# A Fourier mixing and MLP mixer kernel: the setup in a new order

## The chip, the cores and the metric

The kernel runs on one core of a Trainium2 chip. The metric is the device time of one execution in microseconds (us); the shown time is the median of several. The core has five engines that work side by side, each through its own instructions in order: TensorE (PE in the profile, with PEld for its weight loads), VectorE (DVE), ScalarE (ACT), GpSimd (POOL) and SyncE (SP). PE writes its products to PSUM, a small memory of which a DVE or ACT instruction carries them to SBUF, where all tiles lie. Transfers between SBUF and HBM are issued by POOL (with a cast from fp32 to fp16 here) or by SP.

## What is computed

```python
def _attn_ref(x):                      # x: 8 x 3008 x 256
    X = np.fft.fft(x, axis=1)
    X = np.fft.fft(X, axis=2)
    return X.real.astype(np.float32)

def _moe_ref(x, w_tok1, w_tok2, w_ch1, w_ch2):
    xt = x.transpose(0, 2, 1)
    h = np.maximum(xt @ w_tok1, 0.0) @ w_tok2
    u = x + h.transpose(0, 2, 1)
    h2 = np.maximum(u @ w_ch1, 0.0) @ w_ch2
    return (u + h2).astype(np.float32)
```

For each of 8 batches the input (3008 tokens by 256 features) goes through a two-dimensional Fourier transform, of which the real part is kept. The result goes through a token MLP (3008 to 256 to 3008, ReLU between) with a residual, and a channel MLP (256 to 1536 to 256) with a residual.

## The kernel before

**The stages of a batch.** The transform over 3008 = 47 x 64 tokens and 256 features is done by matmuls with tables of cosines and sines. `load_x` brings a batch to SBUF as `xp`, and its mirror image, by two gathers with computed row numbers, as `xm`. `fold` (DVE) adds and subtracts the mirrored halves, so that real tables suffice: xp += xm, then `eo`. It does so in four pieces of four token positions; feature 0 has two operations of its own (L426, L427). `front` is the rest of the Fourier stage and the token MLP. First `pz` (tables `t1n`, `t1b`, copied to `z`), then twelve groups of `pw` (tables `td0`, `td1`, combined to `w`), then `tok1` for each half of the 256 hidden tokens (`pt`, against `hp` and `hq`), then `third`: the last Fourier stage, by the tables `tp` and `tq`, in three chunks of 512 tokens, giving `yt`. Last `pu`, the second token matrix, whose sum with `yt` is `ut`, the input of the channel MLP. `mm1` (`pc`, copied to `c1` with the ReLU) and `mm2` (`po`, or `px` and `py` with sums of blocks that save a matmul) are the channel MLP. SP turns `ut` for the residual (`rt`) and stores the output `osb`.

**The order is written by hand.** The program has a manual schedule: each engine gets its instructions in the order of the program text. `front` and `fold` are generators, and `take(g, n)` puts the next n pieces of one into the text. After the setup a loop over batches and chunks weaves the channel MLP of one batch with the `front` of the next and the `fold` of the one after that. The lists `plan`, `own_plan` and `fold_at` say how many pieces go where.

**The setup.** Before the loop there is a stretch of some 38 us in which all tables are computed on the chip, the weights arrive, batch 0 is folded and taken through its `front`, and the first token matrix is carried into the transform's domain: `carried` multiplies `w1p` and `w1m` by the turned tables (`tts_p`, `tts_q`) and gives `hp` and `hq` (`ph`). This is the part of interest:

- POOL's iotas give `pcol` (the partition number), `ix8f`, `krow`, `kb` and `jrow`. `krow` and `kb` are generated between the two gathers of batch 0, `jrow` behind them.
- DVE makes from `pcol` a set of one-column values (`reff`, `offp`, `offq` and others). With them `kb` becomes the arguments of the angle tables, reduced to a period (`reduced`: add and subtract 2 to the 23rd). ACT takes the sines. `tp` (from `mp`) is reduced on DVE. `tq` (from `mq`) and the `td` tables (from `md`) are begun on ACT, by Identity with a scale and a bias, and ended by one DVE operation each (on `vq` and `vd`).
- `turn` transposes a table on PE, with copies on ACT to `tt`; `turn_rows` reverses its rows with a matmul by `anti` (`pr`), again copied by ACT.
- `filler(n)` issues n matmuls of 128 columns on PE whose result nobody reads.
- The weights follow batch 0 on POOL's queue: `w1p`, `w1m` twice, `w2s` (w_tok2), `wc1` (w_ch1, once straight and once by a gather with the index `ixc`); after the setup come batch 1 (`load_x(1)`) and last `wc2` (w_ch2, `load_wc2`).

At the end of the setup, these are the lines that set the order:

```python
    turn(tp, tts_p, 8)
    table3(tq, vq)
    turn_rows(tts_p, 1.0, 0)
    pieces = fold(0, [nc.vector] * 4)
    take(pieces, 3)
    table_d()
    take(pieces, 9)
    turn(tq, tts_q, 4)
    own = front(0)
    take(own, 4)
    turn_rows(tts_q, -1.0, 24)
```

`relu(0, tok1(0))`, `tok1(1)` and `third(0, ...)` are the three pieces of `front` between the pw groups and the first `pu`. `tok1(0)` also contains a small matmul with `perm` (L492), whose result ACT writes into column 131 of `w`; `third` reads this column.

Of the kernel before, what the change touches and what calls it, by code (L numbers as in the profile page):

```python
# [40 lines left out]
def kernel(  # L41
# [61 lines left out]
    iota(ix8f[:], [[376, BB], [1, 2]], 374, 0)  # L103
    rowi = pvec("rowi")
# [5 lines left out]
    ixc = const.tile([P, 1], I32, tag="ixc")  # L110
    cfeat = pvec("cfeat")
    ts(cfeat[:], pcol[:], 1.0, AT.is_lt, -128.0, AT.mult)
    ts(cfeat[:], cfeat[:], 256.0, AT.add)
    nc.vector.tensor_tensor(out=ixc[:], in0=cfeat[:], in1=pcol[:], op=AT.subtract)
# [7 lines left out]
    def load_x(b, between=(None, None)):  # L122
# [10 lines left out]
        for k in range(2):  # L133
            if between[k] is not None:
                between[k]()
            gather(xmf[:, 8 * D * k:8 * D * (k + 1)], x8, ix8[0:KG, b, k:k + 1])
# [9 lines left out]
    krow = gen.tile([P, 4, 24], FP32, tag="krow")  # L146
    jrow = gen.tile([P, 129], FP32, tag="jrow")
    kb = gen.tile([P, 768], FP32, tag="kb")

    def rows1():  # L150
        iota(krow[:], [[0, 4], [1, 24]], 0, 0)

    def rows3():
        iota(kb[:].rearrange("p (g k) -> p g k", g=NG), [[2, NG], [47, 64]], 0, 0)


# [4 lines left out]
    for t in (tp, tq):  # L161
        for i in range(2):
# [9 lines left out]
    x_tiles = {0: load_x(0, (rows1, rows3))}  # L172
    iota(jrow[:], [[1, 129]], 0, 0)
# [23 lines left out]
                                   op0=AT.mult, op1=AT.add)  # L197

# [38 lines left out]
    def reduced(m, period, nrow, width, eng=nc.vector):  # L237

        v = gen.tile([P, width], FP32, tag="gv", bufs=2, name="gv")[0:nrow, :]
        eng.tensor_scalar(out=v, in0=m, scalar1=1.0 / period, scalar2=TWO23,  # L240
                          op0=AT.mult, op1=AT.add)
        eng.tensor_scalar(out=v, in0=v, scalar1=-TWO23, scalar2=-float(period),
                          op0=AT.add, op1=AT.mult)
        r = gen.tile([P, width], FP32, tag="gr", bufs=2, name="gr")[0:nrow, :]
        eng.tensor_tensor(out=r, in0=v, in1=m, op=AT.add)
        return r

    def sin(out_, in_, scale):
        nc.scalar.activation(out=out_, in_=in_, func=AFT.Sin, scale=scale)

    def table3(tab, r):
        for i in range(2):
            h = slice(64 * i, 64 * i + 64)
            sin(tab[h, :, h], r[h, :].rearrange("p (g k) -> p g k", g=NG), PI2 / S)
# [25 lines left out]
    def filler(n):  # L280
        pw = ps_out("filler")
        for _ in range(n):
            nc.tensor.matmul(pw[:, 0:P], lhsT=ident[:], rhs=anti[:], start=True,  # L283
                             stop=True)
# [9 lines left out]

    mask0, q24 = pvec("mask0"), pvec("q24")
# [4 lines left out]
    m1 = gen.tile([P, 120], FP32, tag="m1")  # L300
    kf = krow[:].rearrange("p a k -> p (a k)")
    ts(m1[0:KR, 0:48], kf[0:KR, 0:48], qcol[0:KR, :], AT.mult, 47 / 4, AT.add)
    ts(m1[0:KR, 48:96], kf[0:KR, 48:96], qcol[0:KR, :], AT.mult)
    ts(m1[0:KR, 96:120], kf[0:KR, 0:24], q24[0:KR, :], AT.mult, 47 / 8, AT.add)
    r1 = reduced(m1[0:KR, :], 47, KR, 120)
    cs = gen.tile([P, 120], FP32, tag="cs")
    sin(cs[0:KR, :], r1, PI2 / 47)

    up, down = pvec("up"), pvec("down")
    nc.vector.memset(up[:], TWO23)
    nc.vector.memset(down[:], -TWO23)
    mp, mq, vq = (gen.tile([P, 768], FP32, tag=n, name=n) for n in ("mp", "mq", "vq"))
    for o, i, scale, bias in ((mq, kb, reff[:], offq), (vq, mq, 1.0 / S, up),
                              (vq, vq, 1.0, down)):
        nc.scalar.activation(out=o[:], in_=i[:], func=AFT.Identity, scale=scale,
                             bias=bias[:])
    ts(mp[:], kb[:], reff[:], AT.mult, offp[:], AT.add)  # L320
    table3(tp, reduced(mp[:], S, P, 768))

    ident = const.tile([P, P], FP16, tag="ident")
    anti = const.tile([P, P], FP16, tag="anti")
    acol = pvec("acol")
    ts(acol[:], pcol[:], -1.0, AT.mult, 127.0, AT.add)
    ts(ident[:], jrow[:, 0:P], pcol[:], AT.is_equal)
    ts(anti[:], jrow[:, 0:P], acol[:], AT.is_equal)

    csv = cs[0:KR, 0:96].rearrange("p (a b k) -> p a b k", a=2, b=2)  # L330
    for i, m in ((0, mask0), (1, xicol)):
        ts(t1n[:, :, i, :], csv[:, :, i, :], m[0:KR, :], AT.mult)
    ts(t1b[:, 1, :], cs[0:KR, 96:120], float(np.sqrt(0.5)), AT.mult,
# [392 lines left out]
    def take(g, n):  # L726
        for _ in range(n):
            next(g, None)
# [132 lines left out]
```

## Time and profile before

| | |
|---|---|
| median of 6 runs | 610.98 us (610.37 to 612.6) |
| the profiled execution | 610.4 us |
| its span, first to last instruction | 608.6 us |
| mean granted PE clock | 0.999 |
| PE busy | 588.2 us (97%) |
| DVE busy | 453.6 us (75%) |
| ACT busy | 442.2 us (73%) |
| POOL busy | 150.5 us (25%) |
| first matmul of PE | 11.69 us after the start of the span |
| first matmul of the second Fourier stage (pw) of batch 0 | 24.99 us |
| HBM read, written | 34.98 MB, 24.64 MB |

Times in the profile are counted from the first instruction of the profiled execution (the span's start); this execution took 1.8 us more than its span. An engine's busy time says little by itself: what counts is which engine others wait for. So the profile also has, for each group of instructions, the idle time of its engine just before it and what ended that ("<-ACT tp L249": until that instruction of ACT was done), and the chain of work that ended last, followed back from the end. "L249" is line 249 of the kernel. A line can be that of a helper: all `tensor_scalar` instructions made through `ts` have L87 or L89, all copies made through `copy` L288 or L290.

### The profile page before, as it was taken

The page shows a single profiled execution, that of the slowest core. Times are in us where ns is not written, and L with a number is a line of the kernel's source. Part 1 is how long each engine was busy: PE and PEld are TensorE (multiplying, and loading weights), DVE is VectorE, ACT ScalarE, POOL GpSimd, SP SyncE. Part 2 cuts the span into 40 slices and gives each one's busy share as a digit, 9 for nine tenths or more (in the row PEclk, how much of TensorE's full clock was granted, in tenths as well). Part 3 has the DMA queues.
Part 4 walks back from the last instruction along what each step waited for, and adds up shares of the span by engine and source line. Part 5 has one row for each costly group of instructions (what it writes and reads, how often), then busy time and mean ns, then how long its engine had stood idle before and what let it go on. Part 6 is the DMA issues. An engine that isn't in the chain of part 4 may idle for free.

```text
span 608.6 us, 15700 instructions
## 1 busy us (share of the span) xinstructions
PE 588.2 (97%) x6322; PEld 422.1 (69%) x6322; DVE 453.6 (75%) x1014; ACT 442.2 (73%) x996; POOL 150.5 (25%) x235
## 2 busy tenths in 40 slices
PE   2899999999999999999999999999999999999996
PEld 1766667666777668767777767766687667766675
DVE  8669679658987697757988688846979676666672
ACT  8866886677768777687777777677776877767672
POOL 8500423112243113401314222311131112111131
PEclk9999999999999999999999999999999999999999
DMA  8994963735548423672329333392231423242423
GB/s 139 210 192 89 180 74 67 150 55 86 62 80 155 84 53 73 112 125 53 84 57 174 57 86 72 70 185 53 53 70 48 95 53 81 61 70 60 90 58 100
DMA packets 86601, 56.53 MB, mean 93 GB/s; under 512 B 54864, under 2 KB 83472, under 8 KB 85776
## 3 DMA queue, kind: packets, MB, share of 16 engines
q1 hardware_dynamic: 78048, 37.84, 32.2%
q0 software_dynamic: 8256, 17.49, 16.7%
q8 instruction: 49, 0.80, 0.5%
q10 hardware_dynamic: 224, 0.20, 0.1%
q14 instruction: 24, 0.20, 0.1%
HBM read 34.98 MB, written 24.64 MB: 98 GB/s over the span
## 4 chain that ended last, share of the span: by engine, by line
PE 92%; DVE 4%; ACT 3%; issue 1%; DVEq 0%; POOL 0%; POOLq 0%
PE pc L592 39%; PE px L633 23%; PE py L633 9%; PE pu L552 7%; PE po L690 4%; PE pt L488 3%; PE pz L445 2%; PE py L519 1%; PE pq L519 1%; PE pw L472 1%; PE pw L473 1%; DVE sb L609 1%; PE filler L283 1%; DVE w L475 1%; DVE xp L423 0%
## 5 line engine op out<-in xcount | busy, mean ns | idle before, releaser
L595 ACT ACTIVATE c<-pc 128x512 f16<-128x512 f32 (+1 forms) x572 | 295.8, 594 | 39.5 <-PE pc L592 19.9
L618 POOL TENSOR_TENSOR osb<-osb,rt 128x256 f32<-128x256 f32 x84 | 81.2, 966 | 377.3 <-DVE osb L618 360.6
L592 PE MATMUL pc<-ut,wc1p 128*128 128x512 f16 x576 | 140.3, 379 | 0.0
L633 PEld LDWEIGHTS <-c 128*128 128x128 f16 x2016 | 121.4, 98 | 20.4 <-DVE c L609 0.3
L592 PE MATMUL pc<-ut,wc1m 128*128 128x512 f16 (+1 forms) x576 | 134.9, 370 | 0.0
L560 DVE TENSOR_TENSOR ut<-pu,yt 128x512 f16<-128x512 f32 (+1 forms) x96 | 64.6, 674 | 51.3 <-PE pu L552 51.1
L633 PEld LDWEIGHTS <-sb 128*128 128x128 f16 x1512 | 89.8, 98 | 10.3 <-issue 0.7
L638 ACT ACTIVATE m<-px 128x256 f32<-128x256 f32 x126 | 48.5, 385 | 66.1 <-PE px L633 38.0
L592 PEld LDWEIGHTS <-wc1p 128*128 128x128 f16 x576 | 52.2, 98 | 49.0 <-issue 2.2
L592 PEld LDWEIGHTS <-wc1m 128*128 128x128 f16 x576 | 53.0, 98 | 46.4
L633 PE MATMUL px<-wst,c 128*128 128x128 f16 x1008 | 70.8, 219 | 0.2 <-DVE c L609 0.2
L633 PE MATMUL px<-wc,c 128*128 128x128 f16 x1008 | 63.1, 219 | 0.0
L290 ACT ACTIVATE z<-pz 128x480 f16<-128x480 f32 (+1 forms) x60 | 40.0, 672 | 18.0 <-PE pz L445 11.0
L609 DVE TENSOR_TENSOR sb<-sb,c 128x768 f16<-128x768 f16 x84 | 50.3, 598 | 2.9
L618 DVE TENSOR_TENSOR osb<-py,m 128x256 f32<-128x256 f32 x84 | 35.2, 420 | 21.9 <-ACT m L638 20.0
L609 DVE TENSOR_TENSOR sb<-c 128x768 f16<-128x768 f16 x84 | 48.9, 582 | 2.3 <-ACT c L595 2.3
L475 DVE SCALAR_TENSOR_TENSOR w<-alt,pw 128x131 f16<-128x131 f16 x96 | 33.1, 350 | 22.9 <-ACT w L290 22.4
L552 PE MATMUL pu<-w2p,uu 128*128 128x512 f16 (+1 forms) x168 | 50.0, 379 | 0.0
L609 DVE TENSOR_TENSOR sb<-c,sb 128x768 f16<-128x768 f16 x84 | 47.1, 561 | 0.0
L609 DVE TENSOR_TENSOR c<-c 128x768 f16<-128x768 f16 x84 | 46.6, 554 | 0.0
L526 DVE TENSOR_TENSOR yt<-py,qs 128x512 f16<-128x512 f32 x48 | 30.9, 686 | 14.3 <-ACT qs L522 14.2
L633 PE MATMUL py<-wst,sb 128*128 128x128 f16 x504 | 35.2, 219 | 0.2 <-DVE sb L609 0.2
(163 smaller groups left out, 687.7 us busy)
## 6 DMA issues: line engine op xcount, KB each, us to landing
out_dram<-osb SPq DMA_DIRECT2D x83, 256.0 KB, 3.5
xp<-in_x_dram POOLq DMA_DIRECT2D x16, 272.0 KB
out_dram<-osb SPq DMA_DIRECT2D x11, 192.0 KB, 3.2
xp<-in_x_dram POOLq DMA_DIRECT2D x16, 127.5 KB
rt<-ut SPq DMA_TRANSPOSE x96, 3.6
w2s<-in_moe_w_tok_dram POOLq DMA_DIRECT2D x1, 1504.0 KB
w1p<-in_moe_w_tok_dram POOLq DMA_DIRECT2D x2, 384.0 KB
wc<-in_moe_w_ch_dram POOLq DMA_DIRECT2D x1, 768.0 KB
```

Source lines behind the costliest of these rows:

```text
L290: nc.scalar.activation(out=out_, in_=in_, func=AFT.Copy)
L475: nc.vector.scalar_tensor_tensor(out=w[:, g, 0:131], in0=alt[:], scalar=pw[:, 131:132], in1=pw[:, 0:131], op0=AT.mult, op1=AT.add)
L526: nc.vector.tensor_tensor(out=yt[:, h, CW * c:CW * c + CW], in0=py[:], in1=qs[:], op=op)
L552: nc.tensor.matmul(pu[:, 0:n], lhsT=uu[:, th, int(minus), h, :], rhs=w2_cols(b, c)[:, th], start=(th == 0), stop=(th == 1))
L560: nc.vector.tensor_tensor(out=ut[:, h, 0:n].rearrange("p (a b) -> p a b", b=64), in0=pu[:, 0:n].rearrange("p (b a) -> p a b", b=64), in1=y ...
L592: nc.tensor.matmul(pc[:, 0:n], lhsT=wc[:, h, ct * P:(ct + 1) * P], rhs=ut[:, h, 0:n], start=(h == 0), stop=(h == 1))
L595: nc.scalar.activation(out=c1[:, ct, 0:n], in_=pc[:, 0:n], func=AFT.Relu)
L609: nc.vector.tensor_tensor(out=o, in0=x, in1=y, op=op)
L618: eng.tensor_tensor(out=o, in0=x, in1=y, op=AT.add)
L633: nc.tensor.matmul(o[:, t], lhsT=a(k)[:, f:f + P], rhs=w(k), start=(first and t == 0 and k == 0), stop=(k == HC - 1), skip_group_check=True)
L638: nc.scalar.activation(out=m[:, i], in_=pa[:, 0], func=AFT.Copy)
L690: nc.tensor.matmul(po[0:n, o:o + D], lhsT=c1[:, ct, ks * P:ks * P + n], rhs=wc2[:, ct, :], start=(ct == 0), stop=(ct == NCT - 1))
```

## The change

The setup is re-planned in these points:

- `krow` and `kb` are gone. `jrow` (0 to 128) is generated ahead of batch 0's transfers, and all tables are computed from it: `mp` by one `scalar_tensor_tensor` from two broadcast inputs, `mq` by ACT as `mp` plus a column `dq`. The gathers follow each other without an iota between them.
- `md` and `vd` are computed and reduced on DVE instead of ACT; `table_d()` goes ahead of the turning, so that ACT has the sines of `cs`, `tp`, `tq` and `td` one behind the other.
- `fold` begins with the two operations of feature 0, which read all of `xm` (both gathers). This holds for every batch.
- `turn(tq, ...)` comes behind the first two pieces of `front(0)`. In the copies of batch 0's `z`, one of the second stretch's and one of the third's, and both of the last ones, are on DVE.
- Fillers: none behind `turn_rows(tts_q, ...)` (24 before), none between the pz pieces (4 before), then 8 instead of 12, and 12 instead of 24 at the end.
- For batch 0 the `perm` matmul (`mirrored`) is issued ahead of `tok1(0)`, and `third(0)` stands between `tok1(0)` and `tok1(1)`, with the PSUM tiles of `mirrored` and `tok1(1)` in another pool. The other batches keep the old order.
- `load_wc2()` comes ahead of `load_x(1)`.

```diff
--- before.py
+++ after.py
...
+    jrow = const.tile([P, 129], FP32, tag="jrow")
+    iota(jrow[:], [[1, 129]], 0, 0)
...
-    ixc = const.tile([P, 1], I32, tag="ixc")
-    cfeat = pvec("cfeat")
-    ts(cfeat[:], pcol[:], 1.0, AT.is_lt, -128.0, AT.mult)
-    ts(cfeat[:], cfeat[:], 256.0, AT.add)
-    nc.vector.tensor_tensor(out=ixc[:], in0=cfeat[:], in1=pcol[:], op=AT.subtract)
...
-    def load_x(b, between=(None, None)):
+    def load_x(b):
...
-            if between[k] is not None:
-                between[k]()
...
-    krow = gen.tile([P, 4, 24], FP32, tag="krow")
-    jrow = gen.tile([P, 129], FP32, tag="jrow")
-    kb = gen.tile([P, 768], FP32, tag="kb")
-    def rows1():
-        iota(krow[:], [[0, 4], [1, 24]], 0, 0)
-    def rows3():
-        iota(kb[:].rearrange("p (g k) -> p g k", g=NG), [[2, NG], [47, 64]], 0, 0)
...
-    x_tiles = {0: load_x(0, (rows1, rows3))}
-    iota(jrow[:], [[1, 129]], 0, 0)
+    x_tiles = {0: load_x(0)}
...
-    def reduced(m, period, nrow, width, eng=nc.vector):
-        v = gen.tile([P, width], FP32, tag="gv", bufs=2, name="gv")[0:nrow, :]
-        eng.tensor_scalar(out=v, in0=m, scalar1=1.0 / period, scalar2=TWO23,
-                          op0=AT.mult, op1=AT.add)
-        eng.tensor_scalar(out=v, in0=v, scalar1=-TWO23, scalar2=-float(period),
-                          op0=AT.add, op1=AT.mult)
-        r = gen.tile([P, width], FP32, tag="gr", bufs=2, name="gr")[0:nrow, :]
-        eng.tensor_tensor(out=r, in0=v, in1=m, op=AT.add)
-        return r
-    def sin(out_, in_, scale):
-        nc.scalar.activation(out=out_, in_=in_, func=AFT.Sin, scale=scale)
+    def reduced(v, r, m, period):
+        ts(v, m, 1.0 / period, AT.mult, TWO23, AT.add)
+        ts(v, v, -TWO23, AT.add, -float(period), AT.mult)
+        nc.vector.tensor_tensor(out=r, in0=v, in1=m, op=AT.add)
+    def sin(out_, in_, period):
+        nc.scalar.activation(out=out_, in_=in_, func=AFT.Sin, scale=PI2 / period)
...
-            sin(tab[h, :, h], r[h, :].rearrange("p (g k) -> p g k", g=NG), PI2 / S)
+            sin(tab[h, :, h], r[h, :, :], S)
...
-            nc.tensor.matmul(pw[:, 0:P], lhsT=ident[:], rhs=anti[:], start=True,
+            nc.tensor.matmul(pw[:, 0:P], lhsT=ident[:], rhs=ident[:], start=True,
...
+    dq, r2, r47 = (pvec(n) for n in ("dq", "r2", "r47"))
+    nc.vector.tensor_tensor(out=dq[:], in0=offq[:], in1=offp[:], op=AT.subtract)
+    ts(r2[:], reff[:], 2.0, AT.mult)
+    ts(r47[:], reff[:], float(NQ), AT.mult)
+    gp = gen.tile([P, NG], FP32, tag="gp")
+    mp, vp, mq, vq = (gen.tile([P, NG, 64], FP32, tag=n, name=n)
+                      for n in ("mp", "vp", "mq", "vq"))
+    up, down = pvec("up"), pvec("down")
+    nc.vector.memset(up[:], TWO23)
+    nc.vector.memset(down[:], -TWO23)
+    ts(gp[:], jrow[:, 0:NG], r2[:], AT.mult, offp[:], AT.add)
+    nc.vector.scalar_tensor_tensor(
+        out=mp[:], in0=jrow[:, 0:64].unsqueeze(1).to_broadcast([P, NG, 64]),
+        scalar=r47[:], in1=gp[:].unsqueeze(2).to_broadcast([P, NG, 64]),
+        op0=AT.mult, op1=AT.add)
+    ixc = const.tile([P, 1], I32, tag="ixc")
+    cfeat = pvec("cfeat")
+    ts(cfeat[:], pcol[:], 1.0, AT.is_lt, -128.0, AT.mult)
+    ts(cfeat[:], cfeat[:], 256.0, AT.add)
+    nc.vector.tensor_tensor(out=ixc[:], in0=cfeat[:], in1=pcol[:], op=AT.subtract)
+    for o, i, scale, bias in ((mq, mp, 1.0, dq), (vq, mq, 1.0 / S, up),
+                              (vq, vq, 1.0, down)):
+        nc.scalar.activation(out=o[:], in_=i[:], func=AFT.Identity, scale=scale,
+                             bias=bias[:])
+    ident = const.tile([P, P], FP16, tag="ident")
+    ts(ident[:], jrow[:, 0:P], pcol[:], AT.is_equal)
+    anti = const.tile([P, P], FP16, tag="anti")
+    acol = pvec("acol")
+    ts(acol[:], pcol[:], -1.0, AT.mult, 127.0, AT.add)
+    ts(anti[:], jrow[:, 0:P], acol[:], AT.is_equal)
...
-    m1 = gen.tile([P, 120], FP32, tag="m1")
-    kf = krow[:].rearrange("p a k -> p (a k)")
-    ts(m1[0:KR, 0:48], kf[0:KR, 0:48], qcol[0:KR, :], AT.mult, 47 / 4, AT.add)
-    ts(m1[0:KR, 48:96], kf[0:KR, 48:96], qcol[0:KR, :], AT.mult)
-    ts(m1[0:KR, 96:120], kf[0:KR, 0:24], q24[0:KR, :], AT.mult, 47 / 8, AT.add)
-    r1 = reduced(m1[0:KR, :], 47, KR, 120)
-    cs = gen.tile([P, 120], FP32, tag="cs")
-    sin(cs[0:KR, :], r1, PI2 / 47)
-    up, down = pvec("up"), pvec("down")
-    nc.vector.memset(up[:], TWO23)
-    nc.vector.memset(down[:], -TWO23)
-    mp, mq, vq = (gen.tile([P, 768], FP32, tag=n, name=n) for n in ("mp", "mq", "vq"))
-    for o, i, scale, bias in ((mq, kb, reff[:], offq), (vq, mq, 1.0 / S, up),
-                              (vq, vq, 1.0, down)):
-        nc.scalar.activation(out=o[:], in_=i[:], func=AFT.Identity, scale=scale,
-                             bias=bias[:])
-    ts(mp[:], kb[:], reff[:], AT.mult, offp[:], AT.add)
-    table3(tp, reduced(mp[:], S, P, 768))
-    ident = const.tile([P, P], FP16, tag="ident")
-    anti = const.tile([P, P], FP16, tag="anti")
-    acol = pvec("acol")
-    ts(acol[:], pcol[:], -1.0, AT.mult, 127.0, AT.add)
-    ts(ident[:], jrow[:, 0:P], pcol[:], AT.is_equal)
-    ts(anti[:], jrow[:, 0:P], acol[:], AT.is_equal)
-    csv = cs[0:KR, 0:96].rearrange("p (a b k) -> p a b k", a=2, b=2)
+    m1 = gen.tile([KR, 5, 24], FP32, tag="m1")
+    for a, n, col, off in ((0, 2, qcol, 47 / 4), (2, 2, qcol, 0.0), (4, 1, q24, 47 / 8)):
+        ts(m1[:, a:a + n, :], jrow[0:KR, 0:24].unsqueeze(1).to_broadcast([KR, n, 24]),
+           col[0:KR, :], AT.mult, off, AT.add)
+    cs, v1 = (gen.tile([KR, 5, 24], FP32, tag=n, name=n) for n in ("cs", "v1"))
+    reduced(v1[:], m1[:], m1[:], 47)
+    sin(cs[:], m1[:], 47)
+    reduced(vp[:], vp[:], mp[:], S)
+    table3(tp, vp)
+    nc.vector.scalar_tensor_tensor(out=vq[:], in0=vq[:], scalar=-float(S), in1=mq[:],
+                                   op0=AT.mult, op1=AT.add)
+    table3(tq, vq)
...
-        ts(t1n[:, :, i, :], csv[:, :, i, :], m[0:KR, :], AT.mult)
-    ts(t1b[:, 1, :], cs[0:KR, 96:120], float(np.sqrt(0.5)), AT.mult,
+        ts(t1n[:, :, i, :], cs[:, i:4:2, :], m[0:KR, :], AT.mult)
+    ts(t1b[:, 1, :], cs[:, 4, :], float(np.sqrt(0.5)), AT.mult,
...
-    quarter = pvec("quarter")
-    nc.vector.memset(quarter[:], 64.0)
-    nc.scalar.activation(out=md[:, 0:128], in_=jrow[:, 1:129], func=AFT.Identity,
-                         scale=pcol[:], bias=quarter[:])
-    nc.scalar.activation(out=md[:, 128:255], in_=jrow[:, 1:128], func=AFT.Copy,
-                         scale=pcol[:])
-    for i, scale, bias in ((md, 1.0 / 256, up), (vd, 1.0, down)):
-        nc.scalar.activation(out=vd[:], in_=i[:], func=AFT.Identity, scale=scale,
-                             bias=bias[:])
+    ts(md[:, 0:128], jrow[:, 1:129], pcol[:], AT.mult, 64.0, AT.add)
+    ts(md[:, 128:255], jrow[:, 1:128], pcol[:], AT.mult)
+    reduced(vd[:], md[:], md[:], 256)
...
-    nc.vector.scalar_tensor_tensor(out=vq[:], in0=vq[:], scalar=-float(S), in1=mq[:],
-                                   op0=AT.mult, op1=AT.add)
...
     def table_d():
-        nc.vector.scalar_tensor_tensor(out=vd[:], in0=vd[:], scalar=-256.0, in1=md[:],
-                                       op0=AT.mult, op1=AT.add)
-        sin(td0[:, 2:130], vd[:, 0:128], PI2 / 256)
-        sin(td1[:, 1:P], vd[:, 128:255], PI2 / 256)
+        sin(td0[:, 2:130], md[:, 0:128], 256)
+        sin(td1[:, 1:P], md[:, 128:255], 256)
...
-            tt(out=xp[:, t, 1:D], in0=xp[:, t, 1:D], in1=xm[0:KR, rv, D - 1:0:-1], op=add)
-            yield
-            if t0 == 1:
+            if s == 0:
...
+            tt(out=xp[:, t, 1:D], in0=xp[:, t, 1:D], in1=xm[0:KR, rv, D - 1:0:-1], op=add)
+            yield
+            if t0 == 1:
...
-                copy(b == 0 and t0 < 2 + 5 * half, zo[:, :, :, t0:t0 + 5],
+                copy(b == 0 and half and t0 < 11, zo[:, :, :, t0:t0 + 5],
...
-            copy(b == 0 and half, zo, pz[:, 0:96].rearrange("p (u k) -> p u k", u=4))
+            copy(b == 0, zo, pz[:, 0:96].rearrange("p (u k) -> p u k", u=4))
...
+        def mirrored(pt):
+            nc.tensor.matmul(pt[:, 260:260 + NG], lhsT=perm[:], rhs=w[:, :, 130],
+                             start=True, stop=True)
+            nc.scalar.activation(out=w[:, :, 131], in_=pt[:, 260:260 + NG],
+                                 func=AFT.Copy)
         def tok1(th):
...
-            pt = ps_f("pt1")
+            pt = (ps_f if b or th == 0 else ps_out)("pt1")
...
-            if th == 0:
-                nc.tensor.matmul(pt[:, 260:260 + NG], lhsT=perm[:], rhs=w[:, :, 130],
-                                 start=True, stop=True)
-                nc.scalar.activation(out=w[:, :, 131], in_=pt[:, 260:260 + NG],
-                                     func=AFT.Copy)
+            if th == 0 and b:
+                mirrored(pt)
...
-        relu(0, tok1(0))
-        yield
-        uv1 = tok1(1)
-        yield
-        third(0, (1, uv1))
-        yield
+        if b:
+            relu(0, tok1(0))
+            yield
+            uv1 = tok1(1)
+            yield
+            third(0, (1, uv1))
+            yield
+        else:
+            mirrored(ps_out("pt1"))
+            uv0 = tok1(0)
+            yield
+            third(0, (0, uv0))
+            yield
+            relu(1, tok1(1))
+            yield
...
+    table_d()
     turn(tp, tts_p, 8)
-    table3(tq, vq)
     turn_rows(tts_p, 1.0, 0)
-    pieces = fold(0, [nc.vector] * 4)
-    take(pieces, 3)
-    table_d()
-    take(pieces, 9)
+    take(fold(0, [nc.vector] * 4), 12)
+    own = front(0)
+    take(own, 2)
...
-    own = front(0)
...
-    turn_rows(tts_q, -1.0, 24)
+    turn_rows(tts_q, -1.0, 0)
...
-    filler(4)
-    take(own, 2)
-    filler(12)
+    filler(8)
...
     for g2 in range(2):
...
     take(own, 5)
-    filler(24)
+    filler(12)
+    load_wc2()
...
-    load_wc2()
...
```

More of the change, by code (lines that the diff above doesn't have):

```diff
@@ L422, in fold @@
             rv = slice(16 - t0, 16 - t1 if t1 < 17 else None, -1)
+            if s == 0:
+                tt(out=xp[:, 1:NR, 0], in0=xp[:, 1:NR, 0], in1=xm[0:KR, ::-1, 0], op=add)
+                tt(out=eo[:, :, 0], in0=xp[:, :, 0], in1=xp[:, :, 0], op=add)
             tt(out=xp[:, t, 1:D], in0=xp[:, t, 1:D], in1=xm[0:KR, rv, D - 1:0:-1], op=add)
@@ L425, in fold @@
             if t0 == 1:
-                tt(out=xp[:, 1:NR, 0], in0=xp[:, 1:NR, 0], in1=xm[0:KR, ::-1, 0], op=add)
-                tt(out=eo[:, :, 0], in0=xp[:, :, 0], in1=xp[:, :, 0], op=add)
                 t = slice(0, t1)
```

## The prediction

> **What bounds the kernel.** I read four views: the page's slices, its chain of waits, the list of waits of TensorE (PE), and the timelines of the engines up to 60 us.
>
> ```profile
> PE   2899999999999999999999999999999999999996
> ...
> PE 92%; DVE 4%; ACT 3%; issue 1%; DVEq 0%; POOL 0%; POOLq 0%
> ```
> The first line is PE's busy share in 40 slices of 15.2 us, the second the share of the chain that ended last. PE is saturated from slice 3 on. The waits of PE after 64 us agree; the first of these two lines is the largest of them, and the other is the largest of the start:
>
> ```profile
> PE pt L488 <- DVE w L475: 0.7, 1, 0.7
> ...
> PE pt L265 <- ACT tp L249: 11.7, 1, 11.7
> ```
> (waiter, releaser, us in total, times, longest.) So whatever shortens the start reaches the end whole, and nothing else in this change can bring much: the change adds no arithmetic after the start. The start is a relay of the engines, each in its own order:
>
> ```profile
> 11.69 1.46 PE L265 MATMUL pt<-ident,tp 128*128 128x128 f16 x12 [11.69 <-ACT tp L249]
> 17.17 1.44 PE L265 MATMUL pt<-ident,tq 128*128 128x128 f16 x12 [1.19 <-ACT tt L275]
> 21.43 1.50 PE L283 MATMUL filler<-anti,ident 128*128 128x128 f16 x24
> 24.99 0.23 PE L472 MATMUL pw<-td,z 128*128 128x128 f16 x1
> ...
> 4.33 0.23 DVE L89 TENSOR_SCALAR m<-krow,qcol 94x48 f32<-94x48 f32 x1
> 4.48 1.53 DVE L87 TENSOR_SCALAR m<-krow,qcol 94x48 f32<-94x48 f32 x1
> 10.76 0.95 DVE L353 SCALAR_TENSOR_TENSOR vq<-vq,mq 128x768 f32<-128x768 f32 x1
> 11.63 0.68 DVE L423 TENSOR_TENSOR xp<-xp,xm 94x1020 f16<-94x1020 f16 x1
> ...
> 9.96 1.68 ACT L249 ACTIVATE tp<-gr 64x768 f16<-64x768 f32 x2
> 14.82 1.69 ACT L249 ACTIVATE tq<-vq 64x768 f16<-64x768 f32 x2
> ...
> 29.53 0.92 POOL L118 DMA_INDIRECT xm<-in_x_dram,ix  x1 [5.61 <-DMA w2s<-in_moe_w_tok_dram]
> 31.37 1.11 POOL L140 DMA_DIRECT2D wc<-in_moe_w_ch_dram  x1 [0.91 <-DMA wc1p<-in_moe_w_ch_dram]
> ```
> Columns: start, duration, engine, line, work, idle before it. The mark to beat is 24.99, the first second-stage matmul (pw); from there PE runs without a gap to 34.9, and channel matmuls (pc) start at 38.60 in the chain. Three blocks of fillers lie on that chain: 1.34 us at 21.59, 0.67 at 24.31, 1.34 at 37.26.
>
> **VectorE (DVE) to the first table.** In the new order the index columns come 0.45 us earlier (the three cfeat operations, 1.99 to 2.44, stand behind mp now). offq is issued at 3.67, dq, r2, r47 and two memsets take 0.4, gp 0.24 (a 0.23 row for 48 elements), so mp starts at 4.37. It has two inputs of 768 elements like the vq row: 0.95, not the 0.67 of the old mp; ends 5.3. cfeat x3, ident, acol, anti, two columns: 1.1; three m operations, 0.2 each, and their reduction 0.75 (as 6.07 to 6.80); then the reduction of 768: 0.60 + 0.60 + 0.96. The table's argument is ready at 10.0, against 9.65 before. That is without any stall.
>
> **The disputed cost is a stall.** The second m operation took 1.53 us where an equal one took 0.23; it ended at 6.01, when POOL's kb iota (5.12 to 5.97) ended. At 10.02 t1n took 0.61 and ended with POOL's w1p issue (9.82 to 10.62). The trace thus charges 1.3 + 0.35 us of stalls before the fold. The Trainium skill ("SBUF — State Buffer", section "Who interferes with whom") says that a tensor_scalar in a two-port mode and a GpSimd instruction exclude each other for the whole instruction, descriptor writing included. This speaks against the change: kb is gone, but POOL now issues w1 1.7 us earlier, and from 1.7 to 12.4 us it never rests, so by the rule each of some ten tensor_scalars could be held by up to 0.85 us: 4 us and more. By the row, two of more than a dozen were held, and the gv pair (7.50, 8.10; 0.56 each) ran beside POOL unhurt. I take 0.6 us, nearer the row that was held by a DMA issue (0.35) than that held by an iota; ends 0 and 1.7, and 4 for a rival.
>
> **ScalarE (ACT).** Its clears end at 5.82. mq no longer follows cs, and mp is there: mq, vq, vq from 5.85 to 8.8 (spacings 1.05, 0.97, 0.94), cs to 9.05. tp waits for DVE: 10.0 to 11.7; tq's argument follows at 10.9, so tq directly behind, 11.65 to 13.3, then td0 and td1, 0.5. The four md and vd activations (11.66 to 13.53, 1.9 us) are gone from ACT; DVE gets five operations, 1.4 us, while vd's separate 0.42 and the 0.46 wait before it go. Copies of the turned tp start at 13.8, against 13.44: **the first half of the start does not gain**. pr copies end at 16.8 (18.1 before), as tq is no longer between.
>
> **The fold and PE.** DVE ends md at about 12.85. x0's last gather must be there now, since feature 0 reads all of xm. The bytes moved pass x0's 1.6 MB at about 11.5 to 12 us, and jrow ahead of the DMAs adds some 0.3 (the krow iota, 96 wide, took 0.27); so this new wait is just covered. Behind it on DVE stand all fold pieces, for which PE waits. Feature 0 takes 0.45, a piece 1.4: eleven to fifteen are folded at 16.15, all at 19.05 (18.64 before). PE: pz of t0=11 at 16.2 (cold, about 0.09 each, 0.9), tq turned 17.1 to 18.4; ACT: two z to 18.0, turned tq to 19.5 (20.03 before). Four more pz, z shared by ACT and DVE (0.6 and 0.67 each); pr 20.5 to 21.3, with no 24 fillers behind; the two last z (now DVE, 0.3 each) to 22.2, beside 8 fillers. pw at 22.25: **2.7 us earlier; with the 0.6 of stalls, 2.1**. w1 is needed 0.2 later: the second gather of x1's first pair was issued unhindered at 22.93 behind w1's last landing, and bytes put that at 20.5.
>
> **Between the token halves.** The 48 ph and 24 pw matmuls keep their 6.7 us. mirrored now stands first and needs the last w of DVE (32.04 before, 0.35 after the last ph), so PE waits about 0.4. Then 1.36 + 0.45 + 1.36 us. DVE computes yt (1.29) ahead of the second uv, which costs about what the shorter ACT queue gives; uu's wait ends 4.8 to 5.2 after ph, against 4.6. But yt no longer stands before ut (35.73 to 37.0 before), and 12 fillers instead of 24 (0.67 less) end with ut: pc at 35.9 against 38.60. This part balances; taken as 0, ends -0.5 and +0.6.
>
> **The queues.** SP's order is the same. On POOL each transfer waits for the one eight before it: the two POOL rows above are transfer 19 waiting for 11 (w2s) and 20 for 12 (wc1p). With w_ch2 as 14, x1's gathers become 19 and 20, and the last is issued at about 31.4 instead of 29.5, behind w_ch2's 0.79 MB. w_ch2 was used at 47.91 without a wait, and would be wanted at 45.8; it now lands some 4 us earlier, x1 later, at 44 to 46 by the bytes. The first fold of x1 stood at 47.32, will stand at 45.2, and waits for both gathers: 0 to 1 us. Queued behind it on DVE: the third chunk's ut, the weight sums and osb. ut is wanted four sub-steps later, the sums of L609 two us later (58.1, used at 63.05), so some 3 us of a DVE stall are covered. Price nothing.
>
> **Sum.** 2.1 us off the start. The profiled execution took 610.4 us (span 608.6), so 608.3; the six runs lie at 610.4 (three) and 611.6 to 612.6, median 610.98, which gives 608.9. I say 608.8. 0.2% is 1.2 us, about what can be told from no change.
>
> **Rivals.**
> - A, forecast, 0.64: gain 1.3 to 3.4 us (no stall and 0.6 in the middle part), 607.4 to 609.7.
> - B, 0.20: **DVE takes ACT's place as the bound.** For it: its chain to the fold has hardly a gap, md and feature 0 stand in it, and the argument of tp is later by 0.35 even without a stall. Against: the fillers that leave the chain are sure. With 1.7 us of stalls as before the gain is 1.0: 610.0.
> - C, 0.09: **the port lock.** POOL's unbroken row of DMA issues holds DVE at most tensor_scalars from 4.1 to 12.4 us. Each us of stall moves tp, fold and pw by one; from 2.7 us the gain is gone, at 4.5 the time is 1.8 up: 612.8. Against it: the gv row.
> - D, 0.04: **the clock.** The Trainium skill ("TensorE: Matmul & The Clock Gate", section "Part 1: The HAM clock gate") warns that PE falls to half rate after an idle window of about 3.4 us, and 44 fillers go. The trace shows half rate at first (12 transposes in 1.46, 0.11 each) and full from 20.6 (24 fillers in 1.50, 0.056 each). By the rule a throttled window would cost 1.7; two, 3.4, so 612.3. By the rows the longest new gap is 1.6 us, at uu: nothing.
> - E, 0.03: x1 lands after 48.2, DVE's cover is used up; each further us costs one, and past 51.5 it is slower, about 612.5. Against: the DMA share falls to 0.28 at 48 to 50 us.
> - That the change does not do what it says is excluded: the issue order of every engine shows its moves.
>
> A's own range and B make 607.0 to 611.2; C, D and E, 0.16, are left out. Faster: A and a tenth of B, 0.66; same 0.18; slower 0.16.
>
> **What would show it.** Right: the first PE transposes at 11.5 to 12.5, tp and tq back to back on ACT, pw at 22.3 to 23.5, pc at 35.5 to 37, no new wait of PE behind 40 us, DVE waiting for a DMA at the x1 fold by up to 1 us without PE following. Wrong: transposes after 13 us with long tensor_scalars beside POOL (C); fold waiting for x0's gather; pw matmuls at 0.11 spacing (D); PE idle at 45 to 60 us (E).

## The result, and the profile after

| | before | after |
|---|---|---|
| median | 610.45 us (610.37 to 612.6, 41 runs) | 609.65 us (609.49 to 610.58, 20 runs) |
| the profiled execution, its span | 610.4, 608.6 us | 609.53, 607.8 us |
| PE busy | 588.2 us | 586.1 us |
| first pw of batch 0 | 24.99 us | 23.28 us |

The medians are 0.8 us apart. The ratio, in which every execution counts, is 0.9978, with a 95% interval of 0.9971 to 0.9984: faster, by 1.4 us in the mean (611.12 against 609.74). The two figures differ because the times of before lie on three levels, about 610.4, 611.6 and 612.3 us (18 of the 41 are on the upper two), while 19 of the 20 of after lie between 609.49 and 609.99. Below, kernels made from after are therefore compared with its median, and kernels made from before with the lowest level of before, whose fastest execution took 610.34 to 610.37 us in every series of runs.

The slices of PE and the chain's shares, in the page of after:

```profile
PE   1999999999999999999999999999999999999996
...
PE 91%; DVE 6%; ACT 2%; issue 0%; DVEq 0%; POOL 0%; POOLq 0%
```
PE is as full as before. In the chain DVE has gained two points: more of the path now runs through it. Where, the rest of this part shows. The start first, in the timeline of PE in after (start, duration, engine, line, work, idle before it):

```profile
12.38 1.46 PE L243 MATMUL pt<-ident,tp 128*128 128x128 f16 x12 [12.38 <-DVE md L87]
...
20.89 0.37 PE L424 MATMUL pz<-t1n,eo 94*128 94x96 f16 x5 [0.71 <-DVE z L266]
21.10 0.81 PE L251 MATMUL pr<-tt,anti 128*128 128x512 f16 x3
...
23.28 0.23 PE L451 MATMUL pw<-td,z 128*128 128x128 f16 x1 [0.31 <-DVE z L266]
...
30.38 0.18 PE L463 MATMUL pt<-w,perm 128*128 128x12 f16 x1 [0.24 <-DVE w L454]
...
35.14 0.96 PE L543 MATMUL pu<-w2s,uu 128*128 128x512 f16 x3 [1.15 <-ACT uu L492]
```
PE begins 0.69 us later than before (12.38 against 11.69) and reaches pw 1.71 earlier (23.28 against 24.99): all of it is won behind the transposes. The first y of the third stage's second chunk, at the same point of both programs, starts at 38.26 against 39.96, so **1.70 us** leave the start.

At the end 0.9 us are left. The lead is the difference of the starts of the same PE instruction in the two traces:

| in after, us | 46.20 | 84.95 | 88.78 | 147.78 | 236.25 | 335.27 | 432.94 | 594.57 |
|---|---|---|---|---|---|---|---|---|
| lead, us | 1.71 | 1.70 | 1.48 | 1.41 | 1.19 | 1.04 | 0.87 | 0.88 |

Half of the gain is given back in small steps, the first between 85 and 89 us. The list of PE's waits after 64 us, in after:

```profile
PE pt L473 <- DVE w L454: 0.7, 1, 0.7
PE py L624 <- DVE sb L600: 0.4, 1, 0.4
```
The first is the one shown of before. The second waits 0.4 where the same wait of before (L633 for sb, L609) was 0.2. What DVE did just ahead of it, in before and then in after:

```profile
83.95 0.34 DVE L475 SCALAR_TENSOR_TENSOR w<-alt,pw 128x131 f16<-128x131 f16 x1
84.22 1.68 DVE L423 TENSOR_TENSOR xp<-xp,xm 94x1020 f16<-94x1020 f16 x1
85.93 0.43 DVE L429 TENSOR_TENSOR eo<-xp 94x512 f16<-94x512 f16 x1
86.27 0.34 DVE L475 SCALAR_TENSOR_TENSOR w<-alt,pw 128x131 f16<-128x131 f16 x1
86.54 0.55 DVE L609 TENSOR_TENSOR sb<-c 128x768 f16<-128x768 f16 x1
```
```profile
82.25 0.35 DVE L454 SCALAR_TENSOR_TENSOR w<-alt,pw 128x131 f16<-128x131 f16 x1
82.52 0.22 DVE L402 TENSOR_TENSOR xp<-xp,xm 94x16 f16<-94x16 f16 x1
82.78 1.05 DVE L403 TENSOR_TENSOR eo<-xp 94x17 f16<-94x17 f16 x1
83.70 0.71 DVE L404 TENSOR_TENSOR xp<-xp,xm 94x1020 f16<-94x1020 f16 x1
84.45 0.43 DVE L408 TENSOR_TENSOR eo<-xp 94x512 f16<-94x512 f16 x1
84.79 0.34 DVE L454 SCALAR_TENSOR_TENSOR w<-alt,pw 128x131 f16<-128x131 f16 x1
85.06 0.55 DVE L600 TENSOR_TENSOR sb<-c 128x768 f16<-128x768 f16 x1
```
From `w` to the block sum `sb` it is 2.59 us before and 2.81 after. The two operations of feature 0 (L402, L403) have moved in front of the first piece of the fold, and so in front of the sum that PE waits for. DVE has no idle time there that could take them: the windows of before give it 4.93 us of work in the 5 us from 85 to 90.

### The profile page after: what moved, and what is told of

It is laid out like the page before. It is cut to its first block, busy times and chain, and to the rows that moved or that the text cites. A ratio compares the mean times of both kernels' runs of the same rounds, so it can differ in the third digit from the quotient of the medians.

```text
span 607.8 us, 15617 instructions
## 1 busy us (share of the span) xinstructions
PE 586.1 (96%) x6278; PEld 419.5 (69%) x6278; DVE 456.6 (75%) x1021; ACT 441.2 (73%) x992; POOL 146.7 (24%) x233
## 4 chain that ended last, share of the span: by engine, by line
PE 91%; DVE 6%; ACT 2%; issue 0%; DVEq 0%; POOL 0%; POOLq 0%
PE pc L583 39%; PE px L624 23%; PE py L624 9%; PE pu L543 7%; PE po L681 4%; PE pt L473 3%; PE pz L424 2%; DVE w L454 1%; PE pq L501 1%; PE py L501 1%; PE pw L451 1%; PE pw L452 1%; DVE sb L600 1%; DVE osb L609 0%; DVE hq L266 0%
## 5 line engine op out<-in xcount | busy, mean ns | idle before, releaser
L609 POOL TENSOR_TENSOR osb<-osb,rt 128x256 f32<-128x256 f32 x84 | 80.4, 957 | 378.4 <-DVE osb L609 363.7
L624 PEld LDWEIGHTS <-sb 128*128 128x128 f16 x1512 | 89.9, 98 | 10.6 <-issue 0.7
L609 DVE TENSOR_TENSOR osb<-py,m 128x256 f32<-128x256 f32 x84 | 35.2, 419 | 22.2 <-ACT m L629 17.4
```

What stands on the lines that cost most here:

```text
L609: eng.tensor_tensor(out=o, in0=x, in1=y, op=AT.add)
L624: nc.tensor.matmul(o[:, t], lhsT=a(k)[:, f:f + P], rhs=w(k), start=(first and t == 0 and k == 0), stop=(k == HC - 1), skip_group_check=True)
```

## The experiments

Unless said otherwise a kernel computes all that the reference asks for. In the expectations T1 is the theory that feature 0's new place costs time in every later batch, T3 that the late landing of w_ch2 makes the levels of before, T4 that PE's clock in the start makes them, T5 that the missing fillers are the gain of the start.

**Feature 0 first in batch 0 alone** (on after; in the other batches the two operations stand where before has them):

```diff
-            if s == 0:
+            if s == 0 and b == 0:
...
+            if t0 == 1 and not (b == 0):
+                tt(out=xp[:, 1:NR, 0], in0=xp[:, 1:NR, 0], in1=xm[0:KR, ::-1, 0], op=add)
+                tt(out=eo[:, :, 0], in0=xp[:, :, 0], in1=xp[:, :, 0], op=add)
```


> The changed kernel, but feature 0 is folded first in batch 0 alone; batches 1 to 7 fold it last, as before the change. Theory T1 (the two feature-0 operations, moved ahead of the block sums in a stretch where DVE is saturated, cost PE a little in every batch): the lead of 1.7 us at 85 us is kept to the end, so about 608.8 us, 0.8 below the changed kernel; PE's wait for sb at about 85 us is 0.16 instead of 0.38. Rival T2 (the lead is lost because the whole steady state sits at another phase to POOL and the transfers): about 609.6, no difference.

Measured: 608.65 us (608.61 to 608.81, 6 runs), ratio 0.9956 [0.9942, 0.9971]: 1.0 us under after. Its lead over before is 1.61 us at 40 us and still 1.60 at 595. The wait for the block sum, in its list of PE's waits after 64 us, is that of before again:

```profile
PE py L627 <- DVE sb L603: 0.2, 1, 0.2
```

**The same place in before** (for the batches from 2 on, so that the start is untouched):

```diff
+            if s == 0 and b >= 2:
+                tt(out=xp[:, 1:NR, 0], in0=xp[:, 1:NR, 0], in1=xm[0:KR, ::-1, 0], op=add)
+                tt(out=eo[:, :, 0], in0=xp[:, :, 0], in1=xp[:, :, 0], op=add)
...
-            if t0 == 1:
+            if t0 == 1 and b < 2:
```


> The kernel before with one part of the change alone: from batch 2 on, feature 0 is folded first. T1: the fast level of 610.4 rises by about 0.8 us, to 611.2. T2: unchanged at 610.4.

Measured: 611.31 us (611.23 to 613.48, 12 runs), ratio 1.0007 [0.9996, 1.0019], with all levels together. Its lowest level is at 611.23 where that of before is at 610.34, 0.9 us more. In the traces its lag behind before grows from 1.14 us at 86 us, all of it lost in the start, to 2.01 at 594. Undone in after it wins 1.0, done in before it loses 0.9: the place of two short operations is shown to be what takes back the gain.

This kernel's profiled execution fell on an upper level (612.43 us), and so shows where a level begins. Its PE, and under it that of before, both from 20.57 us:

```profile
20.57 0.56 PE L449 MATMUL pz<-t1n,eo 94*128 94x96 f16 x5 [0.33 <-ACT z L290]
20.93 1.48 PE L273 MATMUL pr<-tt,anti 128*128 128x512 f16 x3
22.21 1.86 PE L283 MATMUL filler<-anti,ident 128*128 128x128 f16 x24
```
```profile
20.57 0.38 PE L445 MATMUL pz<-t1n,eo 94*128 94x96 f16 x5 [0.33 <-ACT z L290]
20.78 0.81 PE L273 MATMUL pr<-tt,anti 128*128 128x512 f16 x3
21.43 1.50 PE L283 MATMUL filler<-anti,ident 128*128 128x128 f16 x24
```
Up to 20.57 they agree within 0.01. Then the matmuls of one go at full rate and those of the other at half rate, through pr and into the fillers; 1.14 us are lost, about the step from 610.4 to 611.6.

**The order of w_ch2 and batch 1 alone.** In before w_ch2 put ahead:

```diff
+    load_wc2()
     if BB > 1:
         x_tiles[1] = load_x(1)
-    load_wc2()
```


> The kernel before with one part alone: w_ch2 is queued ahead of batch 1. The runs of the kernel before lie at 610.4 or at 611.6 to 612.6; those of the changed kernel at 609.5 to 610.0. Theory T3 (the upper level comes from w_ch2 landing last, later than PE wants it at 47.9 us): all runs at 610.4. Rival T4 (it comes from the start's phase against PE's clock gate, or from elsewhere): both levels as before.

and in after put back:

```diff
-    load_wc2()
     if BB > 1:
         x_tiles[1] = load_x(1)
+    load_wc2()
```


> The changed kernel with batch 1 queued ahead of w_ch2, as before the change. T3: PE wants w_ch2 1.7 us earlier than in the kernel before, at 46.2 us, so it waits for it in the profile, by 0 to 2 us, and the time is 610 to 612. T4: about 609.6, no wait of PE at 46 us.

Measured: 610.41 us (610.36 to 612.43, 12 runs, of which 5 over 611), ratio 0.9995 [0.9983, 1.0007], and 609.63 us (609.47 to 610.82, 12 runs), ratio 0.9976 [0.9966, 0.9985]. The levels stay in the first and do not return in the second, and `po` at 46.14 us in the second has no wait. This part of the change is worth nothing either way, and T3 falls.

**The old fillers in after** (40 of the 44 that the change takes out; the 4 between the pz pieces stay out):

```diff
-    turn_rows(tts_q, -1.0, 0)
+    turn_rows(tts_q, -1.0, 24)
...
-    filler(8)
+    filler(12)
...
-    filler(12)
+    filler(24)
```


> The changed kernel with the fillers of before: 24 behind the reversed tq, 12 (for 8) ahead of pw, 24 (for 12) ahead of pc. Theory T5 (at full clock the fillers lie on the path, since PE's in-order queue holds the last pz behind them): pw 1.3 us later, pc another 0.4 to 0.6 later, so 611.2 to 611.6 us, and a second level of runs 1 us or more above, when PE's clock rises late. Rival T6 (the fillers only fill idle time, and the start's gain comes from the re-planned tables): 609.6 as the changed kernel.

Measured: 611.51 us (611.42 to 611.97, 11 runs), ratio 1.0005 [0.9996, 1.0014]: 1.86 over after. The upper levels that were expected did not come. Its PE:

```profile
22.15 1.50 PE L261 MATMUL filler<-ident 128*128 128x128 f16 x24
...
25.02 0.23 PE L451 MATMUL pw<-td,z 128*128 128x128 f16 x1
```
pw is back at 25.02, where before has it (24.99). But this execution (611.97) is the slowest of the 11, 0.5 over their median, and PE went at half rate until 21.8 us in it, in after only until 19.4. The times are the better measure: 611.51, less the 1.0 of the first experiment and the 0.4 that the move of `third` costs (below), is an estimate of 610.1, which is 0.3 under the lowest level of before. With the old fillers the new tables and the new fold order bring about that much and no more.

**The new fillers in before:**

```diff
-    turn_rows(tts_q, -1.0, 24)
+    turn_rows(tts_q, -1.0, 0)
     take(own, 2)
-    filler(4)
     take(own, 2)
-    filler(12)
+    filler(8)
...
-    filler(24)
+    filler(12)
```


> The kernel before with one part alone: its fillers cut as in the change. T5: the last pz no longer waits for 24 fillers, pw at about 23.8 instead of 25.0, pc some 0.4 earlier again, so 608.8 to 609.3 us: as fast as the whole change, or faster, for lack of the fold's new order. T6: 610.2 to 610.4. In both, the levels of 611.6 to 612.6 shrink towards the lower one if the clock's phase makes them through the fillers.

Measured: 610.48 us (609.41 to 611.84, 12 runs, spread without levels), ratio 0.9989 [0.9978, 1.0001]. At best it wins 1.0, and in the median nothing. The profiled execution (611.43 us) was a bad one:

```profile
20.93 1.48 PE L273 MATMUL pr<-tt,anti 128*128 128x512 f16 x3
...
23.82 1.05 PE L283 MATMUL filler<-anti,ident 128*128 128x128 f16 x8
24.70 0.29 PE L472 MATMUL pw<-td,z 128*128 128x128 f16 x1
```
The eight fillers take 1.05 us, in after 0.62: PE is still at half rate when the second stage begins. The 608.8 to 609.3 that was expected did not come. So neither part makes the gain alone: fewer fillers are worth 1.86 in the new order and 0 to 1.0 in the old one, and the new order with the old fillers about 0.3. That the new order makes the cut pay every time is shown; by what it does so is argued, not shown: in after PE has pz and the turned `tq` from 16.83 to 20.2 without a gap, while in before it waits 1.19 us at 17.17.

**The third stage of chunk 0 behind both halves** (on after, so that batch 0 has the order of the others):

```diff
-            pt = (ps_f if b or th == 0 else ps_out)("pt1")
+            pt = ps_f("pt1")
...
-            if th == 0 and b:
+            if th == 0:
                 mirrored(pt)
...
-        if b:
+        if True:
             relu(0, tok1(0))
```


> The changed kernel with third of chunk 0 behind both token halves in batch 0 too, as before the change. The prediction's balance: 0 (-0.5 to +0.6), so 609.1 to 610.2; if the move itself pays (yt off the way to ut), 610.0 to 610.4; if it costs (DVE computes yt ahead of the second uv), 609.2 to 609.4.

Measured: 609.25 us (609.17 to 609.78, 7 runs), ratio 0.9968 [0.9956, 0.998]: 0.4 under after. The move was a loss. Its PE at the first pu:

```profile
34.43 1.51 PE L543 MATMUL pu<-w2s,uu 128*128 128x512 f16 x4 [0.70 <-ACT qs L504]
```
In after, pu issues one matmul at 33.58 and waits 1.15 us for the second ReLU; here it waits 0.70. In after DVE makes `yt` first (1.29 us, at 32.82) and then, without a pause, the second half's share (`uv`, at 34.08), for which the second ReLU waits.

**Both of these undone** (the first edit and the last one together, on after):

> The changed kernel with the two parts undone that cost time by themselves: feature 0 first in batch 0 alone, third of chunk 0 last in batch 0. If their costs (1.0 and 0.4 us) add, 608.2 to 608.3 us; if they overlap, 608.6.

Measured: 608.25 us (608.22 to 608.61, 5 runs), ratio 0.9962 [0.9949, 0.9975]. It is 1.4 under after: the costs of 1.0 and 0.4 add up.

**The first table's argument reduced at once** (on the first experiment's kernel; `vq` is also ended right behind `anti`, `tq` is turned ahead of pz and reversed behind its first two pieces, and one of the last two z is on ACT):

```diff
+    reduced(vp[:], vp[:], mp[:], S)
+    table3(tp, vp)
     ixc = const.tile([P, 1], I32, tag="ixc")
...
     sin(cs[:], m1[:], 47)
-    reduced(vp[:], vp[:], mp[:], S)
-    table3(tp, vp)
...
-    table_d()
     turn(tp, tts_p, 8)
+    table_d()
     turn_rows(tts_p, 1.0, 0)
+    turn(tq, tts_q, 0)
...
-    turn(tq, tts_q, 4)
+    turn_rows(tts_q, -1.0, 4)
```


> The changed kernel with feature 0 first in batch 0 alone (608.65), and the start in another order: DVE reduces vp directly behind mp, ahead of ident, anti and the small tables, since ACT waited 1.7 us for vp; tq is turned and reversed ahead of its pz pieces, and one of the two last z goes back to ACT. Theory T7 (the table's argument, then ACT's queue, bounds the start): pw at about 21.5 to 22.3 instead of 23.28, so 606.9 to 607.7. Rival T8 (DVE's work up to the end of the fold, 19.9 us, bounds it, and the order on ACT is idle time moved): pw at 23.0 or later, 608.4 to 608.7.

Measured: 608.78 us (608.4 to 610.67, 9 runs), ratio 0.9972 [0.9958, 0.9985], no better than the first experiment, and no longer steady: four of the nine are at 609.83 or more, while the six of the first experiment lie within 0.2 us. In its timeline of DVE:

```profile
12.37 0.24 DVE L87 TENSOR_SCALAR t1n<-cs,mask 94x48 f16<-94x48 f32 x1 [1.15 <-ACT cs L227]
```
ACT now has `tp` and `tq` ahead of the small `cs`, and DVE waits 1.15 us for it in order, with `md` and the whole fold behind. One wait took the place of another. PE, too, waits here ahead of the turned `tq` (1.01 us, at 15.71) and of pz (0.93, at 17.61), so the dense stretch of after is gone. That this brings back the spread fits the two filler runs; it was not tried alone.

**Early matmuls.** If PE's rate in the start makes the levels, work that keeps PE busy from the beginning should remove them. On before, 100 matmuls of a tile of ones, which nobody reads:

```diff
+    ones = const.tile([P, P], FP16, tag="ones")
+    nc.vector.memset(ones[:], 1.0)
...
+    pw0 = ps_out("warm")
+    for _ in range(100):
+        nc.tensor.matmul(pw0[:, 0:P], lhsT=ones[:], rhs=ones[:], start=True, stop=True)
     turn(tp, tts_p, 8)
```


> The kernel before with 100 matmuls of 128 columns, on a tile of ones, ahead of PE's first transpose, in the 11 us in which PE waits anyway. Theory T4 (the levels of 611.6 and 612.2 are runs in which PE reaches full rate after 20 us, by the phase of its clock gate): PE is at full rate by 12 us in every run and stays there through gaps of about 1 us, all runs at 610.3 to 610.5. Rival T9 (the levels have another cause in the start; the late clock is a sign of it): both levels stay.

Measured: 610.91 us (610.36 to 612.47, 12 runs, half of them at 610.4), ratio 1.0004 [0.9993, 1.0015]. The levels stay. Its PE:

```profile
1.05 7.21 PE L734 MATMUL warm<-ones 128*128 128x128 f16 x100 [1.05 <-DVE ones L95]
11.69 1.46 PE L267 MATMUL pt<-ident,tp 128*128 128x128 f16 x12 [3.43 <-ACT tp L251]
...
22.20 2.66 PE L285 MATMUL filler<-anti,ident 128*128 128x128 f16 x24
```
100 matmuls in 7.21 us is 0.072 each, between the two rates: PE did speed up. But after 3.43 us of idle time the transposes take 1.46 as before: it had fallen back. So the run did not set PE's rate in the start, and could not remove the levels. It does show what goes with them. The same trace in stretches of 2 us (the stretch and its length, the busy time of PE, PEld, DVE, ACT and POOL, the granted clock, DMA):

```profile
8.00:10.00 2.00, 0.26 (x5) 0.08 (x2) 1.93 (x6) 1.94 (x4) 2.00 (x4) 1.00 1.08 209
10.00:12.00 2.00, 0.31 (x4) 0.32 (x5) 2.00 (x8) 1.96 (x4) 2.00 (x3) 0.74 0.83 131
...
22.00:24.00 2.00, 2.00 (x18) 1.80 (x17) 0.00 (x0) 1.16 (x3) 1.61 (x3) 0.50 1.09 226
24.00:26.00 2.00, 1.94 (x28) 1.69 (x25) 0.89 (x2) 0.20 (x1) 0.00 (x0) 0.85 0.97 202
```
PE is at half rate from 10.95 us to 24.60. This execution is on the uppermost level (612.29). Its 24 fillers take 2.66 us for 1.50, and the pz behind them begins at 24.70 for 22.77: 1.93 us, the whole step from 610.4 to 612.3. In before the granted clock reads 1.00 in the whole start, although its matmuls go at half rate; here, where the rate had changed before, the half rate is seen. So the mean clock of each of the twelve executions can be set beside its time: it is 0.993 to 0.997 in the six at 610.4, 0.992 in the two at 611.4, and 0.987 in the four from 612.1 up. The longer PE stays at half rate, the higher the level.

The same 100 matmuls on the kernel with both moves undone:

> The same with the 100 matmuls on ones ahead of the first transpose. T4: the upper runs go, and a little more where matmuls ran at half rate up to 20 us, so 607.9 to 608.3. If ACT's and DVE's queues bound the start at any clock: 608.2 to 608.3, with less spread.

Measured: 608.85 us (608.61 to 608.9, 6 runs), ratio 0.9971 [0.9959, 0.9982]: 0.6 slower than without them, which was not expected. Here too they are followed by 3.43 us of idle time and transposes at half rate (1.46). Set beside the trace without them, 0.2 us are lost in the start (pw at 23.44 for 23.22) and 0.35 just before the last block of matmuls (`po`, at 597.07 for 596.51), where PE now waits 0.25 for `osb`. Why stays open.

Last, all together: early matmuls, tables first, both moves undone, and `md` reduced ahead of `t1n`, so that DVE does not wait for `cs`:

```diff
     sin(cs[:], m1[:], 47)
+    md, vd = (gen.tile([P, 255], FP32, tag=n, name=n) for n in ("md", "vd"))
...
+    reduced(vd[:], md[:], md[:], 256)
     for i, m in ((0, mask0), (1, xicol)):
```


> The order with the tables first, mended: md reduced ahead of t1n (DVE waited 1.15 us for cs there, and the fold began at 14.55), third last, and the 100 matmuls. T7 with a full clock: fold begins at 13.4, pw at 21.5 to 22.3, so 606.5 to 607.3 us in all runs. T8: pw at 23.0 or later, 608.2.

Measured: 607.45 us (606.92 to 609.25, 6 runs, four of them up to 607.51), ratio 0.9955 [0.9942, 0.9969]. Its median is the lowest of all kernels here, 2.2 under after, though its times scatter more than those with both moves undone alone. Of the 2.2, 1.4 are the two moves; which of the other parts brings the 0.8 was not tried one by one. Its PE and its DVE:

```profile
10.36 0.84 PE L245 MATMUL pt<-ident,tp 128*128 128x128 f16 x12 [1.27 <-DVE m L89]
...
22.29 0.23 PE L455 MATMUL pw<-td,z 128*128 128x128 f16 x1 [0.23 <-DVE z L268]
```
```profile
13.88 0.23 DVE L403 TENSOR_TENSOR xp<-xp,xm 94x16 f16<-94x16 f16 x1 [0.23 <-DMA xm<-in_x_dram,ix]
```
With only 1.27 us of idle time the transposes run at full rate (0.84) and pw comes at 22.29. It does not last: PE then waits 1.45 us, and from 12.7 to 16.1 us it is at half rate again. A next bound of the start is in the second fence: the fold waits, by 0.23 us, for batch 0's mirror image to land.

## Why the prediction was right, and where not

The sign, the place of the gain and the range were right (609.65 against 608.8, range 607.0 to 611.2); of the predicted 2.1 us, 1.7 appeared in the start and 0.9 at the end. That 609.65 still falls within rival A (607.4 to 609.7) is in part luck: it is at A's edge, and near the 610.0 of rival B, for a cost that neither has.

- **The stall of DVE, 0.6: right in its size.** `tp` could start at 10.63 (predicted 10.6), the turned copies at 14.48 (14.4). In the rows the reductions of `v` and `vp` and the pair of `m` took 0.1 to 0.4 us more than their like. The two that lost most ended with an issue of POOL, as the row of before had: one `m` at 7.21 (w1p's issue at 7.20), the second `v` at 8.09 (w1m's at 8.05). Most of the others ran beside POOL at their usual length. So the rule on the shared port shows in two rows and not in all, and rival C (2.7 and more) did not come. Of rival B, the order came and the size did not: ACT waits 1.72 us for DVE's `vp` ahead of `tp`, but the stalls were 0.6, not 1.7.
- **"The first half of the start does not gain": right.** The transposes come 0.69 later, and with the old fillers in after all that the new order brings is about 0.3.
- **"The fillers that leave the chain are sure": right in after, wrong as a law.** 40 of them are worth 1.86 there; in before, with its gap ahead of the turned `tq`, the cut gives 0 to 1.0. Rival D asked whether PE falls back to half rate in after. It did not; the half rate that costs time is that of the start, and it costs most in before.
- **The end of the fold and the last two z: a term too small.** All was folded at 19.92 (predicted 19.65 with the stall), and the two z, priced at 0.3 each, took 1.01 together, since they stand behind the last pz. That makes pw 23.28 instead of 22.85, the 0.4 missing from the start.
- **Between the token halves: "this part balances; taken as 0" was right as a sum and not in its parts.** The lead is 1.71 us at pw and 1.70 at the third stage. The wait of `mirrored` was 0.24 for 0.4. But the move of `third` alone costs 0.4, as its own run shows. What made up for it is the 12 fillers less in the same stretch: with 24 again, in the run of the old fillers, pw to the first pc takes 14.00 us, in after 13.33.
- **The queues: right.** The first fold of x1 (45.63) has no wait at all, and the two runs with w_ch2's place alone show nothing. Rival E fails.
- **The step that failed: "nothing else in this change can bring much: the change adds no arithmetic after the start".** That is true and not enough. The change also moves two operations in every later batch, and they pass a sum that PE waits for, on an engine that is full there. I had listed that wait of PE among the small ones (0.2 us), and did not ask what the change puts in front of its releaser. The cost was 0.2 us at first and 0.8 to 1.0 over the batches, as the two runs of feature 0 show.

The levels of before are explained in part. An execution is on an upper level when PE reaches full rate late: at 22.95 us in the trace of before with feature 0 first, at 24.60 in the one with early matmuls. On the lowest level it was at 20.6 in before and at 15.8 in before with w_ch2 ahead, which makes no difference, since PE then waits longer for ACT (1.6 us ahead of pz for 0.33). In the kernels with the new order and without early matmuls or tables first, it was at 19.0 to 21.8, and the executions of each lie within about 0.6 us, but for two (610.58 in after, 610.82 with w_ch2 put back). What puts the change of rate early or late was not set by any run. The Trainium skill ("TensorE: Matmul & The Clock Gate", section "Part 1: The HAM clock gate") gives a free-running window of 3.4 us as what decides. The traces agree on the window: wherever PE's rate changed more than once in the start, the stretches between were of 3.41 us or a whole multiple of it (6.83, 13.65), and the changes fall at other times in each execution. They differ on the idle window of about 3.4 us after which PE is said to fall back (rival D): no single pause of that length is needed. With the tables first PE was at full rate from 14.5 us and at half rate from 17.9, though no pause was longer than about 1 us; in those 3.41 us it was busy for 1.5.

## What to carry to other kernels

A change meant for one stage has to be read for every pass of the loop: ask of each moved instruction what it now stands in front of, on an engine that is full, and who waits for that. Idle matmuls that are to keep PE at full rate stand in PE's own order and cost time there; 40 fewer were worth 1.86 us where real work came early and dense, and 0 to 1.0 where it did not. Cut them together with the gaps that they were to bridge. When two moves lie in one stretch, a sum that comes out right may hide a loss: only each move alone shows its sign.

## What the runs showed of the hardware

- PE, sped up by 100 matmuls, was at half rate again after 3.43 us of idle time (12 transposes in 1.46 us) and at full rate after 1.27 us (0.84). In the second case it fell back soon after, at 12.7 us: in the 3.41 us before that it was busy for 1.3, between pauses of 1.27 and 1.45. The granted clock in the windows of before is 1.00 throughout its start, although its matmuls went at half rate until about 20 us; only the spacing of the matmuls shows that. Where PE had changed its rate before, as with the early matmuls, the windows show the half rate (0.50).
- A DVE operation was stretched where POOL's addition `osb` (two inputs from SBUF) ran beside it: the addition of xp and xm to 1.68 us for 0.68 in before, and eo of 17 elements (both inputs xp) to 1.05 for 0.24 in after; they ended 0.6 and 0.1 us after POOL's. The Trainium skill ("SBUF — State Buffer", section "Who interferes with whom") says that an operation with two SBUF inputs contends with a GpSimd instruction that reads SBUF. The change moved this stall from one operation to another and left its length about the same.
